# Top-32 attention feeding a relu-squared MLP on one core: how a block's scores lie in PSUM, which queue first loads k, and the numbers of the planner

## The chip, the core and the metric

The kernel runs on one core of a Trainium2 chip. Its engines work in parallel and wait for each other by semaphores: TensorE (PE in the profile, PEld its weight loads), VectorE (DVE), ScalarE (ACT), GpSimd (POOL) and the queue that issues most DMAs (SP). The metric is the device time of one execution in microseconds (us), lower is better.

## The reference

For 8 batches and 8 heads, with 576 positions of 64 values, attention keeps for each query only the 32 highest scores. A two-layer MLP follows on the 4608 tokens.

```python
scores = scale * np.matmul(q, k.transpose(0, 1, 3, 2))            # 576 x 576 for each head
kth = np.partition(scores, -top_k, axis=-1)[..., -top_k:-top_k + 1]
scores = np.where(scores >= kth, scores, -1000000000.0)
attn = np.exp(scores - np.max(scores, axis=-1, keepdims=True))
attn = attn / (np.sum(attn, axis=-1, keepdims=True) + 1e-09)
attn_out = np.matmul(attn, v)
...
h = x @ w_in                                                      # 4608 x 512 by 512 x 2048
return (np.maximum(h, 0.0) ** 2) @ w_out                          # 4608 x 2048 by 2048 x 512
```

## The kernel before

Attention is cut into 144 blocks. A block has 128 queries of two heads (or the last 64 queries of four heads, group Z) against all 576 keys, so 1152 scores per partition, in the order of `batch_order`. Each block goes through these steps; the letters are the names of the tiles in the profile.

- TensorE transposes the q and k of a head pair (`rq`, `rk`) and ScalarE copies them to `qk`. This is done once per pair.
- TensorE computes the scores into three PSUM banks `ss` (L408 is the line of every matmul, L411 of every transpose). The keys and queries of the first head lie in partitions 0 to 63, those of the second in 64 to 127, so the two heads use two halves of the array's rows. The 1152 scores lie in the three banks without a gap. The middle bank therefore holds the first head's last 64 scores beside 448 of the second head's. The matmul for these 64 is an operation of its own (`PIECES[1]`), and waits until the other four have ended.
- ScalarE copies all 1152 scores to SBUF in one instruction (`s`, L504). VectorE then takes the larger of each two scores that are half a row apart (`m`, L558), one from PSUM, the other from the copy. After that PSUM is free. There is one such `ss` for all blocks, so the next block's scores wait for this block's `m`.
- VectorE and GpSimd find the 32nd largest score (`kth`), working through maxima, minima and sums of pairs: `t` and `f` (L555) on GpSimd, `f`, `c` and `kth` (L563, L578, L582, L585) on VectorE.
- ScalarE builds a mask `w` (L593), TensorE transposes scores and mask (`ident,s` and `steep_bf,w`, 4 and then 5 chunks), and ScalarE takes the exponential (`p`, L626).
- TensorE multiplies with v (`vb,p`), ScalarE copies the result (`av`, L652), VectorE takes the reciprocal of the sums (`rzall`, L654), GpSimd scales (`x`, L656), TensorE transposes it (`ident_bf,x`) and ScalarE copies it to `xt`.

When a chunk of 128 to 512 tokens is complete, `feed` runs the MLP for it: `xt,win` on TensorE, relu and square on ScalarE or GpSimd (`g`), `wo,g` on TensorE, a copy `o` and a store. The MLP of a batch runs beside the attention of the next. The last chunks, two of 128 tokens, can only run at the end.

No order is written by hand. Every operation is given to `Plan.op` with an assumed duration and a priority, and `schedule` plays the program through with these numbers: an engine that is free takes the ready operation of the lowest priority. The order in which each engine's operations start in that play is the order of its instructions. `verdict` and a second program `again` behind a branch are not taken with these inputs.

Of the kernel before, what the change touches and what calls it, by code (L numbers as in the profile page):

```python
# [5 lines left out]
ALU = mybir.AluOpType  # L6
# [70 lines left out]
class Op:  # L77
    __slots__ = ("eng", "dur", "prio", "fn", "deps", "tiles", "takes", "n", "users", "start", "end",
                 "idx", "sem", "val", "ndma", "seq", "vc", "waits", "wars", "later", "nbf", "lk")
# [5 lines left out]
class Plan:  # L85
# [3 lines left out]
    def op(self, eng, dur, prio, fn, r=(), w=(), u=(), hold=(), take=(), after=(), order=(), sem=None, ndma=0, nbf=0.0, lk=False):  # L89
# [4 lines left out]
        o.eng, o.dur, o.prio, o.fn = eng, dur - (.05 if eng == "act" else 0), prio, fn  # L94
        o.sem, o.ndma, o.seq, o.nbf, o.lk = sem, ndma, len(self.ops), nbf, lk
# [22 lines left out]
    def schedule(self, t0=0.0, latency=0.12, own=0.07):  # L118
# [24 lines left out]
        while events:  # L143
            t = events[0][0]
            while events and events[0][0] <= t + 1e-9:
                _, _, kind, x = heapq.heappop(events)
                if kind == "end":
# [7 lines left out]
                    for v in x.users:  # L155
# [3 lines left out]
                        if left[v] == 0:  # L159
                            push(readyat[v], "ready", v)  # L160
# [47 lines left out]
class Emitter:  # L208
# [72 lines left out]
def bass_top_k_attn__then__act_relu_squared_kernel(  # L281
# [32 lines left out]
    STEP = 3.2  # L314

# [97 lines left out]
    def build(full, weights, pl):  # L413
        state = {"n": 0, "u": 0, "last": {}}
# [6 lines left out]
        def load_pair(b, hp, base):  # L421
            rq, rk, rv = tile("rq"), tile("rk"), tile("rv")

            def load(t, src):
                def fn():
                    r = at(t)
                    res = [nc.sync.dma_start(r[:, 0:4, h, :], src[b, 2 * hp + h, 0:512, :].rearrange(
                        "(tb p) d -> p tb d", p=P)) for h in range(2)]
                    res.append(nc.sync.dma_start(
# [14 lines left out]
            pl.op("sp", 2.3, base - 79.9, load(rk, k), w=[rk], take=[rk], sem=slot_sem, ndma=3)  # L444
# [16 lines left out]
            o_q = pl.op("pe", .55, base - 45, t4(tq, rq), r=[rq], w=[tq], take=[tq, qk])  # L461
            pl.op("pe", .55, base - 44.9, t4(tk, rk), r=[rk], w=[tk], take=[tk], order=[o_q])
# [5 lines left out]
            pl.op("gp", .9, base + 5, lambda: gp.tensor_copy(at(vb)[:, :, 0:D], at(rv)[:, :, :]),  # L468
# [3 lines left out]
        def top_k(gi, qks, tg):  # L472
# [461 lines left out]
```

## Time and profile before

| | |
|---|---|
| time, median of 3 runs | 969.63 us (967.36 to 971.03) |
| the profiled execution's own time | 972.14 us |
| its span, first to last instruction | 970.3 us |
| busy: PE, DVE, POOL, ACT | 887.8, 863.3, 750.4, 737.5 us |
| VectorE's first instruction of a block starts at | 15.86 us |
| VectorE's last `kth` ends at | 935.1 us |

The span is what the trace covers; the time also holds what lies around it. A busy TensorE is not TensorE at its peak, since matmuls overlap. The tables of stretches give the busy time of each engine in a piece of the span: an engine whose busy time is that of the piece had no room left.

### The profile page before, as it was taken

What the parts mean: (1) busy time and instruction counts of PE and PEld (TensorE: products, weight loads), DVE (VectorE), ACT (ScalarE), POOL (GpSimd) and SP (SyncE); (2) the same over time, 40 slices, a digit from 0 to 9 for tenths busy, and PEclk for the clock granted to TensorE, in tenths of its full rate; (3) what the DMA queues carried; (4) which work ended last, traced back from release to release, by engine and by line L of the source; (5) the groups of instructions that cost most, each with busy time, mean ns of one, the idle gap of its engine ahead of it and who ended that gap; (6) DMA issues with size and microseconds to landing.
All of it is one profiled execution on the core that took longest, in us unless ns stands there. A gap on an engine that the chain in (4) does not pass through costs nothing.

```text
span 970.3 us, 21522 instructions
## 1 busy us (share of the span) xinstructions
PE 887.8 (91%) x7650; PEld 620.2 (64%) x7650; DVE 863.3 (89%) x3269; ACT 737.5 (76%) x1133; POOL 750.4 (77%) x794
## 2 busy tenths in 40 slices
PE   5877789999799999999998999999999999999995
PEld 3655566777566666666766676666676655666654
DVE  1888799999999999999999999999999999786831
ACT  2555588898789877997789977998788879686752
POOL 5787688788877777778777787778799986599950
PEclk9976799999999999999999999999999999999998
DMA  6541153102310022001221112111111210000011
GB/s 155 143 124 67 44 136 79 38 15 60 87 38 15 20 67 71 16 15 38 59 49 39 39 35 74 25 39 38 36 48 26 53 33 23 23 11 13 22 34 37
DMA packets 126981, 48.15 MB, mean 50 GB/s; under 512 B 119184, under 2 KB 119184, under 8 KB 126864
## 3 DMA queue, kind: packets, MB, share of 16 engines
q1 hardware_dynamic: 126864, 46.69, 18.9%
q8 instruction: 62, 1.02, 0.4%
q14 instruction: 55, 0.45, 0.2%
HBM read 37.22 MB, written 9.44 MB: 48 GB/s over the span
## 4 chain that ended last, share of the span: by engine, by line
PE 44%; DVE 30%; POOL 10%; ACT 8%; issue 6%; DMA 0%; SPq 0%; POOLq 0%; DVEq 0%
PE ps L408 34%; PE ps L411 10%; DVE f L582 8%; DVE c L578 7%; DVE kth L585 6%; POOL f L555 6%; DVE m L558 5%; POOL t L555 3%; DVE f L563 3%; ACT p L626 3%; ACT s L504 2%; ACT w L593 1%; ACT g L706 1%; POOL x L656 1%; DMA rk<-in_k_dram 0%
## 5 line engine op out<-in xcount | busy, mean ns | idle before, releaser
L408 PE MATMUL ps<-qk 64*128 64x512 f32 (+6 forms) x1600 | 281.7, 413 | 30.0 <-DVE m L558 28.3
L408 PEld LDWEIGHTS ps<-qk 64*128 64x128 f32 (+1 forms) x1600 | 178.3, 183 | 141.6 <-DVE m L558 46.5
L582 DVE MATCH_REPLACE8 f<-c,f 128x104 f32<-128x104 f32 (+2 forms) x864 | 268.7, 320 | 0.0
L578 DVE MAX8 c<-f 128x8 f32<-128x104 f32 (+2 forms) x864 | 248.5, 325 | 0.2
L593 ACT ACTIVATE w<-s,kth 128x576 bf16<-128x576 f32 x288 | 220.6, 780 | 16.8 <-DVE kth L585 16.3
L555 POOL TENSOR_TENSOR t<-s 128x576 int32<-128x576 int32 x144 | 201.6, 1411 | 25.2 <-ACT s L504 25.1
L411 PE MATMUL ps<-ident,s 128*128 128x128 f32 x1296 | 204.1, 286 | 6.8 <-ACT w L593 6.3
L504 ACT COPY s<-ps 128x1152 f32<-128x1152 f32 x144 | 161.4, 1121 | 64.1 <-PE ps L408 62.8
L585 DVE MAX8 kth<-f 128x8 f32<-128x576 f32 x288 | 205.1, 751 | 2.4 <-POOL f L555 2.4
L555 POOL TENSOR_TENSOR f<-t,m 128x576 int32<-128x576 int32 x144 | 202.8, 1408 | 0.0
L626 ACT ACTIVATE p<-ps 128x1152 bf16<-128x1152 f32 x144 | 162.9, 1131 | 35.1 <-PE ps L408 34.3
L555 POOL TENSOR_TENSOR f<-t,f 128x288 int32<-128x288 int32 x144 | 114.5, 795 | 85.2 <-DVE f L563 82.6
L411 PEld LDWEIGHTS ps<-ident,s 128*128 128x128 f32 x1296 | 146.4, 144 | 35.5 <-ACT w L593 8.5
L558 DVE TENSOR_TENSOR m<-ps,s 128x576 f32<-128x576 f32 x144 | 107.9, 749 | 45.2 <-ACT s L504 41.9
L408 PE MATMUL ps<-wo,g 128*128 128x512 bf16 x576 | 143.4, 380 | 1.0 <-ACT xt L681 0.4
L408 PE MATMUL ps<-xt,win 128*128 128x512 bf16 (+3 forms) x704 | 134.3, 331 | 4.7 <-ACT xt L680 3.3
L408 PE MATMUL ps<-steep_bf,w 128*128 128x128 bf16 x1296 | 122.5, 223 | 0.0
L555 POOL TENSOR_TENSOR t<-m 128x288 int32<-128x288 int32 x144 | 115.0, 799 | 4.3 <-DVE m L558 4.3
L563 DVE TENSOR_REDUCE f<-m 128x288 f32<-128x576 f32 x144 | 106.4, 752 | 0.2
L706 ACT ACTIVATE g<-ps 128x512 bf16<-128x512 f32 (+1 forms) x152 | 85.3, 576 | 24.4 <-PE ps L408 23.8
L408 PEld LDWEIGHTS ps<-steep_bf,w 128*128 128x128 bf16 x1296 | 99.0, 100 | 3.9
L656 POOL TENSOR_TENSOR x<-av,rzall 128x256 bf16<-128x256 f32 (+1 forms) x88 | 47.1, 535 | 58.6 <-DVE rzall L654 58.2
(56 smaller groups left out, 750.7 us busy)
## 6 DMA issues: line engine op xcount, KB each, us to landing
rq<-in_q_dram SPq DMA_DIRECT2D x64, 128.0 KB, 2.5
rk<-in_k_dram SPq DMA_DIRECT2D x64, 128.0 KB, 2.6
rv<-in_v_dram SPq DMA_DIRECT2D x64, 128.0 KB, 2.4
out_dram<-o SPq DMA_DIRECT2D x31, 256.0 KB, 2.1
g<-in_moe_w_in_dram SPq DMA_DIRECT2D x8, 512.0 KB, 4.5
g<-in_moe_w_out_dram SPq DMA_DIRECT2D x8, 512.0 KB, 4.5
rv<-in_v_dram SPq DMA_DIRECT2D x96, 16.0 KB, 2.2
out_dram<-o SPq DMA_DIRECT2D x10, 128.0 KB, 2.3
```

Source lines behind the costliest of these rows:

```text
L408: return pe.matmul(o, l, r, start=start, stop=stop, skip_group_check=True)
L411: return pe.matmul(o, i, ident, is_transpose=True, skip_group_check=True, **kw)
L504: cp = pl.op("act", 1.15, tg - LEAD + 1, lambda: act.copy(at(st)[:, :, :].rearrange("p i c -> p (i c)"), wide(ss)), r=[ss], w=[st])
L555: return pl.op("gp", dur, prio, lambda: gp.tensor_tensor(o().bitcast(I32), x().bitcast(I32), y().bitcast(I32), op), **kw)
L558: dve(.7, lambda: vec.tensor_tensor(at(m)[:, :, :], wide(ss).rearrange("p (i c) -> p i c", i=2)[:, :, 0:HALF], at(st)[:, :, HALF:S], ALU.m ...
L563: big = dve(.67, lambda: vec.tensor_reduce(at(f)[:, :, 0:QUART], at(m)[:, :, :].rearrange("p i (a c) -> p i c a", a=2), AX.X, ALU.max), dp ...
L578: lambda i=i, t=t, c0=c0, c1=c1: vec.max(eighth(t, i), at(f)[:, i, c0:c1]),
L582: lambda i=i, t=t, c0=c0, c1=c1: vec.match_replace(at(f)[:, i, c0:c1], eighth(t, i), at(f)[:, i, c0:c1], NEG), hold=[f])]
L585: ks.append(chain(kth, i, prev[i] + [low], .665, lambda i=i: vec.max(eighth(kth, i), at(f)[:, i, :]), hold=[f]))
L593: pl.op("act", .77, tw + .8 * i, lambda i=i: act.activation(at(wt)[:, i, :], at(st)[:, i, :], ACTF.Relu, bias=kth[:, i, n:n + 1], scale=-1.0),
L626: pl.op("act", 1.15, tt + 1, lambda: act.activation(at(pt)[:, :, :].rearrange("p k q -> p (k q)"), wide(e), ACTF.Exp, scale=0.125), r=[e], ...
L706: return act.activation(at(g)[:, 0:kf * nt], bank(hh)[:, 0:kf * nt], ACTF.Relu)
```

## The change

The first head's 512 main scores get a bank, the second head's 512 get a bank, and the last 64 scores of both share the third. The four matmuls are now one operation: first the first head's 64 columns, then 512 and 512, then the second head's 64, ahead of which TensorE waits on a semaphore (`fence`) that the first of the four raises. ScalarE's copy becomes two instructions, 1024 and 128 columns, and `m` waits for both. The k of the first head pair is issued from ScalarE's queue. Of the loads, only those of v now wait for the zeroing of `rv`. The assumed durations are new; a reciprocal counts as ready 1.5 us later in the plan (`LATE`); the MLP chunks that wait for the last batch, except the very last one, get a lag of 10 in their priorities (`LAGL`, before 0).

```diff
-                            push(readyat[v], "ready", v)
+                            push(readyat[v] + v.late, "ready", v)
...
+    def via(self, plan, e):
+        for o in plan.order["sp"]:
+            if o.via == e:
+                assert not o.waits
+                for i in o.fn():
+                    i.then_inc(self.sem(o.idx[0]), 16)
+
     def emit(self, plan, e, eng):
         for o in plan.order[e]:
+            if o.via is not None:
+                continue
...
+    LATE = 1.5
+    LAGL = 10
...
+    def two(ap, step, n_):
+
+        return bass.AP(ap.tensor, ap.offset, [ap.ap[0], [step, 2], [1, n_]])
+
+    fence, fences = nc.alloc_semaphore("fence"), [0]
...
-            PIECES = [[(0, 0, 0, 512, True), (1, 576, 512, 64, True), (1, 640, 0, 384, False), (1, 1024, 384, 128, True)],
-                      [(0, 512, 512, 64, False)]]
-
-            def scores(part):
+            def scores():
                 o = wide(ss)
-                for h, to, c0, n_, first in PIECES[part]:
+                for h, to, c0, n_ in ((0, 1024, 512, 64), (0, 0, 0, 512), (1, 512, 0, 512), (1, 1088, 512, 64)):
                     x = at(qks[h])
+                    if to == 1088:
+                        pe.wait_ge(fence, fences[0])
                     ins = mm(o[:, to:to + n_], x[64 * h:64 * h + 64, 0, 128 * gi:128 * gi + 128],
-                             x[64 * h:64 * h + 64, 1, c0:c0 + n_], first)
+                             x[64 * h:64 * h + 64, 1, c0:c0 + n_], to != 1088)
+                    if to == 1024:
+                        fences[0] += 1
+                        ins.then_inc(fence, 1)
                 return ins
...
-            o_s = pl.op("pe", 1.2, tg - LEAD, lambda: fs(0), r=qu, w=[ss], take=[ss, st])
-            pl.op("pe", .15, tg - LEAD, lambda: fs(1), r=qu, w=[ss], after=[o_s])
-            cp = pl.op("act", 1.15, tg - LEAD + 1, lambda: act.copy(
-                at(st)[:, :, :].rearrange("p i c -> p (i c)"), wide(ss)), r=[ss], w=[st])
+            pl.op("pe", 1.25 if gi != Z else 1.4, tg - LEAD, scores if gi != Z else scores_z, r=qu, w=[ss], take=[ss, st])
...
+            cp = [pl.op("act", 1.1, tg - LEAD + 1, lambda: act.copy(
+                two(flat(), 640, 512), two(wide(ss), 512, 512)), r=[ss], w=[st]),
+                pl.op("act", .35, tg - LEAD + 1, lambda: act.copy(
+                    flat()[:, 512:640], wide(ss)[:, 1024:1152]), r=[ss], w=[st])]
...
-                dve(.7, lambda: vec.tensor_tensor(
-                    at(m)[:, :, :], wide(ss).rearrange("p (i c) -> p i c", i=2)[:, :, 0:HALF],
-                    at(st)[:, :, HALF:S], ALU.max), dp=-ME, r=[ss], hold=[st], after=[cp], w=[m], take=[m])
+                dve(.67, lambda: vec.tensor_tensor(
+                    at(m)[:, :, :], two(wide(ss), 736, HALF), two(flat()[:, HALF:], HALF, HALF), ALU.max),
+                    dp=-ME, r=[ss], hold=[st], after=cp, w=[m], take=[m])
...
-            rz = pl.op("dve", .1, tt + 4, lambda: vec.reciprocal(rzall[:, r0:r0 + nu], at(avs)[:, 0:nu, 64]), r=[avs])
+            rz = pl.op("dve", .1, tt + 4, lambda: vec.reciprocal(rzall[:, r0:r0 + nu], at(avs)[:, 0:nu, 64]), r=[avs], late=LATE)
...
-            lag = 0 if last else LAG
+            lag = 0 if end else LAGL if last else LAG
...
-        if o.eng == "sp":
+        if o.eng == "sp" and o.takes and o.takes[0].pool.name == "rv":
             o.deps.update(zeros)
```

The new numbers give every engine a new order. Three places are shown. The first is the start of the program. SP's first rows before (`g` is where a weight waits for its cast, 128x4x64 is the bulk of a q, k or v):

```order
L826 DMA g<-in_moe_w_in_dram 128x1024 x2
L427 DMA rq<-in_q_dram 128x4x64 x2
L429 DMA rq<-in_q_dram 64x2x64
L427 DMA rk<-in_k_dram 128x4x64 x2
L429 DMA rk<-in_k_dram 64x2x64
```

SP's first rows now; ScalarE's now begin with the first three loads of `rk`:

```order
L447 DMA rq<-in_q_dram 128x4x64 x2
L449 DMA rq<-in_q_dram 64x2x64
L456 DMA rv<-in_v_dram 128x4x64 x2
L460 DMA rv<-in_v_dram 64x64 x3
L447 DMA rq<-in_q_dram 128x4x64 x2
```

The two loads of `win` have moved from the first place to behind the fourth head pair, and k has left SP.

The second place is ScalarE between two copies of scores, in the second half of the program as it now stands:

```order
L533 COPY s<-ps 128x2x512
L683 COPY av<-ps 128x260
L535 COPY s<-ps 128x128
L737 ACTIVATE g<-ps 128x512
L624 ACTIVATE w<-s,kth 128x576
```

The small copy need not follow the large one: in 76 of the 144 blocks it does, in 68 something else stands between, mostly one copy to `av` or `xt`; in the 128th block it is 11 instructions, 10 of them of `g`.

The third place is TensorE at the end of the program. Before:

```order
L408 MATMUL ps<-wo,g 128x512 x12
L411 MATMUL ps<-ident_bf,x 128x128
L411 MATMUL ps<-ident,s 128x128 x5
L408 MATMUL ps<-steep_bf,w 128x128 x5
L408 MATMUL ps<-vb,p 128x65 x10
L411 MATMUL ps<-ident_bf,x 128x128
L847 MATMUL ps<-fone 1x3
L408 MATMUL ps<-xt,win 128x128 x64
L408 MATMUL ps<-wo,g 128x512 x16
```

And now:

```order
L428 MATMUL ps<-steep_bf,w 128x128 x5
L428 MATMUL ps<-wo,g 128x512 x4
L428 MATMUL ps<-xt,win 128x128 x16
...
L428 MATMUL ps<-wo,g 128x512 x8
L428 MATMUL ps<-vb,p 128x65 x10
L428 MATMUL ps<-wo,g 128x512 x12
L431 MATMUL ps<-ident_bf,x 128x128
L888 MATMUL ps<-fone 1x3
L428 MATMUL ps<-xt,win 128x128 x64
L428 MATMUL ps<-wo,g 128x512 x16
```

The last block's transposes now stand ahead of the work of the chunk before the last, and twelve `wo,g` stand between the last `vb,p` and the transpose of its result.

## Rows read from the trace of the kernel before

**Rows 1.** Stretches: length; busy PE, PEld, DVE, ACT, POOL; PEclk, DMA share, GB/s.

```profile
16.00:113.00 97.00, 74.61 (x484) 56.93 (x484) 74.43 (x273) 48.81 (x69) 71.23 (x71) 0.81 0.37 99
145.50:824.50 679.00, 645.20 (x5756) 450.33 (x5754) 667.50 (x2539) 570.08 (x872) 546.96 (x555) 1.00 0.17 42
826.00:936.00 110.00, 108.09 (x883) 71.09 (x882) 82.85 (x310) 78.11 (x129) 90.81 (x100) 1.00 0.05 18
```

**Rows 2.** VectorE's waits, 16 to 114 us: us in total, times, longest.

```profile
DVE m L558 <- ACT s L504: 35.5, 10, 15.9
```

**Rows 3.** VectorE's waits, 145 to 826 us.

```profile
DVE rzall L654 <- ACT av L652: 5.1, 12, 0.9
DVE m L558 <- ACT s L504: 2.9, 3, 2.1
```

**Rows 4.** VectorE's waits, 826 to 936 us.

```profile
DVE rzall L654 <- ACT av L652: 11.8, 7, 2.8
```

**Rows 5.** The chain that ended last, its first 22 us: start, length, what.

```profile
4.75 4.66 DMA rk<-in_k_dram
...
11.42 2.52 PE ps L408 x7
...
13.98 0.70 PE ps L408 x2
...
15.86 0.77 DVE m L558
...
19.18 1.45 PE ps L411 x6
```

**Rows 6.** SP's timeline, first us: start, length of the issue.

```profile
0.74 0.87 SPq L826 DMA_DIRECT2D g<-in_moe_w_in_dram  x2
...
4.75 1.66 SPq L429 DMA_DIRECT2D rk<-in_k_dram  x1
```

**Rows 7.** The page's DMA issues: count, KB each, median us to landing.

```profile
rk<-in_k_dram SPq DMA_DIRECT2D x64, 128.0 KB, 2.6
```

**Rows 8.** TensorE's timeline near 891 us, one block's scores: start, length.

```profile
890.64 1.36 PE L408 MATMUL ps<-qk 64*128 64x512 f32 x8
891.94 1.04 PE L408 MATMUL ps<-wo,g 128*128 128x512 bf16 x4
892.90 0.43 PE L408 MATMUL ps<-qk 64*128 64x64 f32 x2
893.26 0.66 PE L411 MATMUL ps<-ident,s 128*128 128x128 f32 x4
```

**Rows 9.** TensorE's groups by shape, 890.6 to 891.1 us: count, busy, mean ns.

```profile
L408 PE MATMUL ps<-qk 64*128 64x512 f32 x1 | 0.7, 693 | 0.0
L408 PE MATMUL ps<-qk 64*128 64x384 f32 x1 | 0.5, 539 | 0.0
```

**Rows 10.** Groups by shape, whole span: busy, mean ns, idle before them.

```profile
L504 ACT COPY s<-ps 128x1152 f32<-128x1152 f32 x144 | 161.4, 1121 | 64.1 <-PE ps L408 62.8
L466 ACT COPY qk<-ps 128x128 f32<-128x128 f32 x32 | 8.8, 274 | 0.1
```

**Rows 11.** Groups by shape, 826 to 970 us.

```profile
L408 PE MATMUL ps<-qk 64*128 64x512 f32 x26 | 14.6, 641 | 0.4 <-DVE m L558 0.4
```

**Rows 12.** Table of stretches round 265 us and 956 us, columns as in rows 1.

```profile
258.00:264.00 6.00, 3.89 (x35) 3.03 (x36) 6.00 (x27) 5.01 (x8) 6.00 (x6) 1.00 0.43 98
264.00:270.00 6.00, 6.00 (x55) 3.54 (x53) 4.54 (x16) 1.39 (x3) 3.98 (x6) 0.72 0.22 48
...
954.00:958.00 4.00, 3.67 (x41) 3.60 (x40) 0.88 (x5) 0.94 (x3) 0.00 (x0) 0.57 0.02 6
```

**Rows 13.** TensorE's timeline at the end: start, length, [idle before, who ended it].

```profile
952.27 0.49 PE L408 MATMUL ps<-vb,p 128*128 128x65 bf16 x10 [1.22 <-ACT p L626]
953.80 0.23 PE L411 MATMUL ps<-ident_bf,x 128*128 128x128 bf16 x1 [1.03 <-POOL x L656]
...
954.49 5.18 PE L408 MATMUL ps<-xt,win 128*128 128x128 bf16 x64
```

More of the change, by code (lines that the diff above doesn't have):

```diff
@@ L78 @@
     __slots__ = ("eng", "dur", "prio", "fn", "deps", "tiles", "takes", "n", "users", "start", "end",
-                 "idx", "sem", "val", "ndma", "seq", "vc", "waits", "wars", "later", "nbf", "lk")
+                 "idx", "sem", "val", "ndma", "seq", "vc", "waits", "wars", "later", "nbf", "lk", "late",
+                 "via")
 ENGS = ("pe", "act", "dve", "gp", "sp")
@@ L87, in __init__, with op @@
         self.ops = []
-    def op(self, eng, dur, prio, fn, r=(), w=(), u=(), hold=(), take=(), after=(), order=(), sem=None, ndma=0, nbf=0.0, lk=False):
+    def op(self, eng, dur, prio, fn, r=(), w=(), u=(), hold=(), take=(), after=(), order=(), sem=None, ndma=0, nbf=0.0, lk=False, late=0.0, via=None):
         o = Op()
-        o.eng, o.dur, o.prio, o.fn = eng, dur - (.05 if eng == "act" else 0), prio, fn
-        o.sem, o.ndma, o.seq, o.nbf, o.lk = sem, ndma, len(self.ops), nbf, lk
+        o.eng, o.dur, o.prio, o.fn = eng, dur - (.1 if eng == "act" else 0), prio, fn
+        o.sem, o.ndma, o.seq, o.nbf, o.lk, o.late, o.via = sem, ndma, len(self.ops), nbf, lk, late, via
         o.takes = list(take)
@@ L443, in load_pair @@
             pl.op("sp", 2.3, base - 80, load(rq, q), w=[rq], take=[rq], sem=slot_sem, ndma=3)
-            pl.op("sp", 2.3, base - 79.9, load(rk, k), w=[rk], take=[rk], sem=slot_sem, ndma=3)
+            via = "act" if not full and not state["pairs"] else None
+            state["pairs"] += 1
+            pl.op("sp", 2.3, base - 79.9, load(rk, k, nc.scalar if via else nc.sync), w=[rk], take=[rk], sem=slot_sem,
+                  ndma=3, via=via)
             pl.op("sp", 2.3, base - 70, loadv, w=[rv], take=[rv], sem=slot_sem, ndma=5)
@@ L487, in scores, with scores_z @@
                     ins = mm(o[:, to:to + n_], x[64 * h:64 * h + 64, 0, 128 * gi:128 * gi + 128],
[L488 removed]
+                             x[64 * h:64 * h + 64, 1, c0:c0 + n_], to != 1088)
+                    if to == 1024:
+                        fences[0] += 1
+                        ins.then_inc(fence, 1)
                 return ins
[L491 removed]
+            def scores_z():
                 o = wide(ss)
[L493 removed]
+                for i in range(2):
@@ L494, in scores_z @@
                     x = at(qks[i])
-                    for h in range(2):
-                        ins = mm(o[64 * h:64 * h + 64, to:to + n_], x[64 * h:64 * h + 64, 0, 512:576],
-                                 x[64 * h:64 * h + 64, 1, c0:c0 + n_], first)
+                    for to, c0, n_, first in ((1024 + 64 * i, 512, 64, i == 0), (512 * i, 0, 512, True)):
+                        for h in range(2):
+                            ins = mm(o[64 * h:64 * h + 64, to:to + n_], x[64 * h:64 * h + 64, 0, 512:576],
+                                     x[64 * h:64 * h + 64, 1, c0:c0 + n_], first)
@@ L709, in feed @@
                 w_ = kf * nt
-                ho = pl.op("pe", kf * 4 * (nt / 2200 + .01), tf + lag, fh, r=[xt], w=[hh], take=[hh, g], after=weights,
+                ho = pl.op("pe", .03 + kf * 4 * (nt / 2340 + .002), tf + lag, fh, r=[xt], w=[hh], take=[hh, g], after=weights,
                       nbf=tf if not last else 0)
@@ L829, in setup, with warm @@
                                  r=[s]))
+        for i in range(int(WARM / .45)):
+            t = Tile(psum)
+            def warm(t=t):
+                for _ in range(2):
+                    ins = mm(bank(t), ident_bf[:, :], ident_bf[:, :].unsqueeze(1).broadcast_to([P, 4, P]), True)
+                return ins
+            pl.op("pe", .45, 1e5, warm, w=[t], take=[t], after=[i2], nbf=.45 * i)
         return [i1], pre, zeros, weights
```

39 lines of the change are left out of this document (20 added, 19 removed).

## The prediction

> **What bounds the kernel now.** I read the table of stretches first, then VectorE's waits in each stretch, then the chain of waits at both ends. The table [rows 1] shows three stages with different limits. From 145 to 824 us VectorE is busy 667.5 of 679.0 us, while TensorE has 34 us to spare: VectorE is the bound, and whatever other engines save there is worth nothing. Its waits there are small: 5.1 us for the result that a reciprocal needs, 2.9 us for a block's scores [rows 3]. From 826 to 936 us it is the other way round: TensorE is busy 108.1 of 110.0 us and VectorE has 27.2 us of holes, because the MLP work of two batches falls in there. From 16 to 113 us neither is full. VectorE has 22.6 us of holes and waits for scores, at a mean granted clock of 0.81 [rows 1, 2]; The longest, 15.9 us, is the wait for the very first block, ahead of 16. The waits of 16 to 113 for scores are therefore 35.5 - 15.9 = 19.6 us in nine pieces.
>
> So the change can win at the start and at the end. In the middle it can only lose.
>
> **The start of the program.** The chain starts with the last piece of k: issued at 4.75 us, landed 4.66 later, at 9.41 [rows 5]. Ahead of it SP issued two loads of 512 KB for the weights [rows 6]. They now come behind the fourth pair, and k's three loads go out on ScalarE's queue beside q's. The two weight loads took 0.87 us to issue, so about 0.45 each; three k loads from about 0.74 on are out by about 2.1. With this start's 4.66 to landing that is 6.8, with the median of 2.6 [rows 7] 4.7. I take 5.7, since q and k still move together and only the weights are gone: **-3.7 us** (bounds -2.6 and -4.7).
> [...]
> ScalarE's other first work, a table load, is pushed back behind the three issues by these 1.35 us; it is covered by the wait for the landing, and would cost that much without it. The MLP first uses the weights some 20 blocks later in TensorE's order, so their delay is covered by those blocks.
>
> **A block's scores.** At the end of the program one block's four matmuls take 1.36 us. The fifth, alone, takes 0.43, and 0.36 from its start to that of the next work [rows 8]. At half the clock, at the start, the fifth takes 0.70 on the chain [rows 5]. Does the new group stay at 1.36? In the old one the first head streams 512 columns and the second 64 + 384 + 128 = 576; in the new one each has 576. If the two heads' matmuls overlap as now, the longer half is what it was, and the group is unchanged. That they overlap, rows 9 show: in the first half microsecond there is one pass of the first head's 512 columns (each fp32 matmul is two) and already a pass of the second head's 384, which the program issues later. I take 1.36. The other bound is no overlap at all, at most twice that. The semaphore ahead of the last 64 is raised by the first and shortest matmul, so it should be up long before its turn: nothing, since the two 512s cover it. Without that cover all that stands behind on TensorE would wait too.
>
> **ScalarE's copy.** 1152 columns take 1121 ns, 128 take 274 [rows 10]. A straight line between them gives 1015 for 1024, so the two copies take 1289, **0.17 us more per block**, 24 us of ScalarE's time in all. In the middle ScalarE is busy 570 of 679 us [rows 1] and VectorE waits for scores in three places only, so I cost it at nothing there. At the start it lies on the chain. The first block's `m` thus moves from 15.86 by -3.7 - 0.70 + 0.17, to 11.6: **-0.5** beside the -3.7.
>
> **The other holes of the start.** Nine waits for scores remain. Each had the fifth matmul at up to 0.70 in it, less 0.17 for the copy, so 4.8 us. In some, the next pair's transposes (1.45 us at 19.18, [rows 5]) stood between the four matmuls and the fifth. They can't any more; I count two of them, 2.9. Together **-8 us**. The bounds are -3, if only half of the fifth matmuls lay on the path and no transposes, and -15, if most of the 19.6 vanishes.
>
> **The middle.** A later reciprocal can win at most the 5.1 us [rows 3]. What is late next is `x` on GpSimd, and then the MLP, which has a lag of its own in the plan. Against that stands a fuller ScalarE and a TensorE with more holes. I take **-2** (bounds -5 and +6).
>
> **The end.** Of 512-column passes 26 remain after 826 us [rows 11], so 13 blocks, each 0.36 less on a full TensorE: **-4.7** (bounds 0 and 13 x 0.43 = -5.6). VectorE's 11.8 us of waits for reciprocals there [rows 4] are no term of their own, since TensorE sets the pace. Behind the last block TensorE stood still for 1.22 and 1.03 us [rows 13]. Then the clock fell (0.57 in that stretch, [rows 12]), and 64 matmuls of the last chunk took 5.18. The new order puts twelve `wo,g` into the second gap and the last transposes earlier, so that exponential and result are covered. I take **-2.5**: 2.25 of gap and something of the clock (bounds 0 and -3.5).
>
> **The sum.** -3.7 - 0.5 - 8 - 2 - 4.7 - 2.5 = -21.4 us. The profiled execution's own time, 972.14, would become 950.7. That execution lies 2.5 us over the median of the runs shown; from the median, 969.63, it is **948 us**. Adding the bounds gives -34 to about +0, so 935 to 969.
>
> **The rivals.**
> *More is won* (933 us): the fifth matmul is gone from every loop in which scores wait for `m` and `m` for scores, so the start follows VectorE almost at once. For it: 19.6 us of waits in nine places. Against it: the half clock there. The sum at its bounds, 969.6 - 34 = 935, and a little of the 27.2 us of holes at the end. Chance 0.15.
> [...] Chance 0.14. [...]
> *The heads don't overlap* (960 us): with the first head's 64 and 512 ahead of the second's 512, the second could wait until the first head's second pass has started. The group then grows by one pass, at most 0.69 [rows 9], and eats the 0.43; only the load, the reciprocals and the last order are left, some 9 us. Against it: rows 9. Chance 0.08. [...]
> *Slower* (976 us): ScalarE becomes what VectorE waits for. In 68 blocks an instruction stands between the two copies, so `m` is later by up to 0.17 + 0.38 or more, `ss` stays taken as long, and everything behind `m` on VectorE waits. To cancel the win it takes 21.4 us, or 0.2 us of VectorE's time in each of the 110 or so blocks of the middle; 976 needs 0.25. For it: in the middle ScalarE has only 109 us left of 679. Against it: three waits for scores there, 2.9 us. Chance 0.06.
>
> **Chances.** Forecast 0.57 (its own range 940 to 956), more 0.15, clock 0.14, no overlap 0.08, slower 0.06. The range that leaves out no more than 2 in 10 is 934 to 962. A measurement of this kernel tells about 0.5% from no change, 4.8 us. Under 964.8: the forecast, the win and nearly all of the two at 960, so 0.89; within 0.5%: 0.06; slower 0.05.
>
> **What would show it.** Right: the first `m` near 11.6 us; one group of eight passes per block, 1.3 to 1.4 us at full clock; holes of VectorE from the first `m` to 113 us near 14 us; VectorE busy 98% or more of the middle, as now; TensorE full from about 815 us and the last gaps gone. Wrong: a score group of 1.8 or more; `m` waiting for the second copy in dozens of places; granted clock at half in stretches of the middle; first `m` after 13 us.

## The result, and the profile after

The changed kernel takes **933.08 us** (median; 930.32 to 938.05) beside 970.33 for the kernel before on the same chip: a ratio of 0.9627 [0.9577, 0.9676], 37 us less. The profiled execution is the shortest of its four, 930.32 us with a span of 928.2, so a stretch of it can flatter the change by a few us; where it does, other kernels with the same start stand beside it. Ratios leave out four executions at a lower granted clock (one of e2 at 0.958, one of e8 at 0.648 and 1187 us, two of e11 at 0.959 and 0.958), and the medians hold them.

The first part of the page of the changed kernel; 77 of its 7330 matmuls are missing from the record, so that TensorE's busy time is some us too low:

```profile
PE 810.1 (87%) x7253; PEld 565.7 (61%) x7330; DVE 864.2 (93%) x3269; ACT 742.8 (80%) x1277; POOL 750.3 (81%) x794
```

VectorE has as much to do as before (863.3), TensorE some 64 us less than its 887.8 (a kernel that differs only in the lag, e5 below, has a full record with 823.3), in a span that is 42 us shorter. The table of stretches of the changed kernel, for the cuts of [rows 1]; the third, where VectorE finishes, now lies 36 us earlier:

```profile
16.00:113.00 97.00, 69.72 (x620) 53.72 (x620) 93.67 (x356) 66.15 (x109) 89.96 (x91) 0.91 0.52 137
145.50:824.50 679.00, 609.33 (x5532) 423.58 (x5594) 673.22 (x2547) 578.56 (x990) 550.25 (x560) 0.99 0.17 42
790.00:900.00 110.00, 106.51 (x917) 70.91 (x929) 92.44 (x352) 84.37 (x155) 98.48 (x110) 1.00 0.05 18
```

VectorE's holes between 16 and 113 us fell from 22.6 to 3.3 us. In the middle VectorE was the bound and still is; TensorE's busy time there fell by 36 us (62 of the missing matmuls lie there), which buys nothing. At the end TensorE is still the bound (106.5 of 110), but VectorE gets through more blocks in the same time (92.4 busy, before 82.9).

Equal cuts of time hold different blocks. So the next two tables are cut at the same blocks (counted from 0): from the start of the `m` of block 0 to that of block 16, from there to block 120, and from there to the end. Before:

```profile
15.86:125.50 109.64, 83.66 (x576) 63.44 (x576) 87.01 (x321) 57.10 (x79) 81.78 (x82) 0.83 0.36 96
125.50:748.10 622.60, 589.26 (x5325) 417.71 (x5326) 614.80 (x2345) 522.78 (x798) 504.16 (x512) 1.00 0.19 46
748.10:970.30 222.20, 208.00 (x1728) 134.53 (x1725) 161.43 (x605) 153.80 (x253) 157.22 (x169) 0.99 0.10 27
```

And after:

```profile
12.39:102.70 90.31, 63.70 (x534) 49.08 (x535) 85.32 (x317) 57.68 (x94) 83.22 (x84) 0.91 0.51 133
102.70:725.70 623.00, 552.72 (x5097) 390.96 (x5149) 619.56 (x2347) 532.72 (x915) 507.49 (x514) 0.99 0.19 47
725.70:928.20 202.50, 187.83 (x1604) 121.51 (x1626) 159.32 (x607) 148.51 (x264) 154.44 (x166) 0.99 0.08 24
```

That is the whole account of the two profiled spans, which lie 42 us apart (the medians 37): 3.5 us up to the first `m`, 19.3 in the first 16 blocks, nothing in 104 blocks of the middle, 19.7 in the last 24 blocks and what follows them.

VectorE's waits after, 16 to 114 us, to be read beside [rows 2] (of which 19.6 us lie in this stretch):

```profile
DVE m L589 <- ACT s L535: 2.6, 4, 1.4
DVE f L613 <- POOL f L586: 2.3, 1, 2.3
```

145 to 826 us, beside [rows 3]; the waits for reciprocals are gone:

```profile
DVE f L613 <- POOL f L586: 3.1, 5, 1.5
DVE m L589 <- ACT s L535: 1.9, 4, 0.8
```

The chain of waits of the changed kernel up to its first `m`, beside [rows 5]:

```profile
1.79 3.89 DMA rq<-in_q_dram
...
5.82 1.96 PE ps L431 x8
...
7.79 0.58 ACT qk L488
...
8.60 2.55 PE ps L428 x6
...
11.17 1.01 ACT s L533
12.18 0.18 ACT s L535
...
12.39 0.77 DVE m L589
```

The last piece is now one of q. It landed at 5.68 us, 3.73 earlier than k's did. But all eight large transposes now stand behind that landing, where before those of q ran while k was on its way: from landing to scores it takes 2.92 us instead of 2.01. Before, the four of the first q began 1.35 us ahead of k's landing at 9.41:

```profile
8.06 1.12 PE L411 MATMUL ps<-ident,rq 128*128 128x128 f32 x4 [8.06 <-DMA rq<-in_q_dram]
```

TensorE's timeline near 601 us, one block's scores and the next work, beside [rows 8]:

```profile
600.82 1.34 PE L428 MATMUL ps<-qk 64*128 64x64 f32 x8
602.09 0.66 PE L431 MATMUL ps<-ident,s 128*128 128x128 f32 x4
```

All eight passes take 1.34 us, 1.27 to the start of the next work. Before it was 1.30 and then 0.36 for the fifth matmul: 0.39 us a block less. The first tenth of a microsecond, 600.80 to 600.90, by shape, beside [rows 9]:

```profile
L428 PE MATMUL ps<-qk 64*128 64x512 f32 x1 | 0.7, 693 | 0.0
L428 PE MATMUL ps<-qk 64*128 64x64 f32 x1 | 0.3, 320 | 0.0
```

A pass of 512 columns already runs beside the first pass of the first head's 64. I take it for the second head's: the second pass of the 64 starts only in the next tenth, and the first head's own 512 stands behind that one in the program. e6, which holds the second head back, fits: there the group takes 3.02 us. ScalarE's two copies in the groups by shape (busy, mean ns, idle before them), beside [rows 10]:

```profile
L533 ACT COPY s<-ps 128x1024 f32<-128x1024 f32 x144 | 146.5, 1017 | 84.2 <-PE ps L428 83.8
L535 ACT COPY s<-ps 128x128 f32<-128x128 f32 x144 | 40.7, 282 | 0.0
```

The end of TensorE's timeline after, beside [rows 13]:

```profile
910.24 0.48 PE L428 MATMUL ps<-vb,p 128*128 128x65 bf16 x10
910.55 2.75 PE L428 MATMUL ps<-wo,g 128*128 128x512 bf16 x12
913.14 0.22 PE L431 MATMUL ps<-ident_bf,x 128*128 128x128 bf16 x1
914.07 0.19 PE L888 MATMUL ps<-fone 128*1 128x3 f32 x2 [0.71 <-ACT o L768]
914.19 3.75 PE L428 MATMUL ps<-xt,win 128*128 128x128 bf16 x64
```

The gaps of 1.22 and 1.03 us have become one of 0.71, and the last 64 matmuls take 3.75 us instead of 5.18.

### The profile page after: what moved, and what is told of

Same layout as the page of the kernel before. It is cut to its first block, busy times and chain, and to the rows that moved or that the text cites. A ratio compares the mean times of both kernels' runs of the same rounds, so it can differ in the third digit from the quotient of the medians.

```text
span 928.2 us, 20946 instructions
## 1 busy us (share of the span) xinstructions
PE 810.1 (87%) x7253; PEld 565.7 (61%) x7330; DVE 864.2 (93%) x3269; ACT 742.8 (80%) x1277; POOL 750.3 (81%) x794
## 4 chain that ended last, share of the span: by engine, by line
DVE 45%; PE 35%; ACT 14%; issue 3%; DMA 1%; POOL 1%; SPq 0%; DVEq 0%
PE ps L428 27%; DVE f L613 13%; DVE kth L616 10%; DVE c L609 10%; PE ps L431 9%; DVE m L589 6%; DVE f L594 5%; ACT p L657 5%; ACT w L624 3%; ACT s L533 2%; ACT g L737 1%; ACT g L751 1%; DMA rq<-in_q_dram 1%; ACT xt L711 0%; ACT qk L488 0%
## 5 line engine op out<-in xcount | busy, mean ns | idle before, releaser
L609 DVE MAX8 c<-f 128x8 f32<-128x104 f32 (+2 forms) x864 | 243.7, 321 | 0.1
L428 PE MATMUL ps<-qk 64*128 64x64 f32 (+3 forms) x1280 | 213.9, 454 | 32.8 <-DVE m L589 31.6
L586 POOL TENSOR_TENSOR t<-s 128x576 int32<-128x576 int32 x144 | 203.1, 1413 | 17.7 <-ACT s L535 17.6
L431 PE MATMUL ps<-ident,s 128*128 128x128 f32 x1296 | 200.2, 283 | 16.0 <-ACT w L624 15.4
L533 ACT COPY s<-ps 128x1024 f32<-128x1024 f32 x144 | 146.5, 1017 | 84.2 <-PE ps L428 83.8
L616 DVE MAX8 kth<-f 128x8 f32<-128x576 f32 x288 | 203.4, 748 | 1.6 <-POOL f L586 1.6
L428 PEld LDWEIGHTS ps<-qk 64*128 64x128 f32 (+1 forms) x1280 | 129.2, 180 | 110.2 <-DVE m L589 48.1
L428 PE MATMUL ps<-xt,win 128*128 128x512 bf16 (+3 forms) x674 | 126.8, 324 | 13.7 <-ACT g L737 7.4
L428 PE MATMUL ps<-wo,g 128*128 128x512 bf16 x529 | 134.2, 379 | 4.5 <-ACT xt L711 1.2
L589 DVE TENSOR_TENSOR m<-ps,s 128x576 f32<-128x576 f32 x144 | 107.5, 747 | 19.3 <-ACT s L535 16.9
L737 ACT ACTIVATE g<-ps 128x512 bf16<-128x512 f32 (+1 forms) x152 | 87.2, 581 | 20.2 <-PE ps L428 19.7
L428 PEld LDWEIGHTS ps<-xt,win 128*128 128x128 bf16 x704 | 57.7, 98 | 51.8 <-ACT g L737 11.8
```

The lines of the kernel that those rows point to most:

```text
L431: return pe.matmul(o, i, ident, is_transpose=True, skip_group_check=True, **kw)
L533: cp = [pl.op("act", 1.1, tg - LEAD + 1, lambda: act.copy(two(flat(), 640, 512), two(wide(ss), 512, 512)), r=[ss], w=[st]), pl.op("act", . ...
L586: return pl.op("gp", dur, prio, lambda: gp.tensor_tensor(o().bitcast(I32), x().bitcast(I32), y().bitcast(I32), op), **kw)
L589: dve(.67, lambda: vec.tensor_tensor(at(m)[:, :, :], two(wide(ss), 736, HALF), two(flat()[:, HALF:], HALF, HALF), ALU.max), dp=-ME, r=[ss] ...
L609: lambda i=i, t=t, c0=c0, c1=c1: vec.max(eighth(t, i), at(f)[:, i, c0:c1]),
L616: ks.append(chain(kth, i, prev[i] + [low], .665, lambda i=i: vec.max(eighth(kth, i), at(f)[:, i, :]), hold=[f]))
```

## The experiments

The theory after the result: the layout is the core, the loads add 3 to 4 us, and the rest of the change only arranges. The rival: the new numbers of the planner carry a good part. This table holds, for each kernel cut at the same blocks as above, the start of the first `m` and the length of the three stretches in its profiled execution, the granted clock of the first stretch, and the median of its runs (us):

| kernel | first `m` | 0 to 16 | clock there | 16 to 120 | 120 to end | time |
|---|---|---|---|---|---|---|
| before | 15.86 | 109.6 | 0.83 | 622.6 | 222.2 | 968 to 970 |
| the change | 12.39 | 90.3 | 0.91 | 623.0 | 202.5 | 933.1 |
| e1, layout only | 15.04 | 96.5 | 0.89 | 620.6 | 215.6 | 946.7 |
| e2, all but the layout | 13.13 | 101.6 | 0.87 | 630.6 | 215.4 | 965.6 |
| e3, old loads | 15.11 | 96.6 | 0.86 | 623.1 | 203.4 | 936.7 |
| e4, `LATE` 0 | 12.68 | 97.8 | 0.84 | 634.3 | 204.1 | 948.6 |
| e5, no lag | 12.64 | 96.7 | 0.86 | 621.5 | 204.8 | 933.3 |
| e6, heads serial | 15.49 | 153.1 | 0.65 | 752.3 | 238.6 | 1158.2 |
| e7, copies adjacent | 12.38 | 96.4 | 0.88 | 627.6 | 203.1 | 936.1 |
| e8, TensorE busy early | 10.65 | 97.6 | 0.79 | 623.2 | 203.0 | 936.6 |
| e9, old durations | 12.62 | 91.3 | 0.91 | 619.3 | 215.7 | 943.0 |
| e10, `LATE` 3 | 12.47 | 96.1 | 0.84 | 632.2 | 203.1 | 947.3 |
| e11, serial fifth | 13.12 | 116.3 | 0.74 | 643.1 | 214.0 | 979.8 |
| e12, `LATE` 1.7 | 12.45 | 97.0 | 0.84 | 623.3 | 206.4 | 941.5 |

Each stretch comes from one execution. In the first 16 blocks the change and e9 have the highest granted clock, 0.91, and take 90 and 91 us; the seven others with the new layout and without added matmuls or waits were granted 0.84 to 0.89 and take 96 to 98.

**e1: the layout alone**, with the kernel before's loads and planner.

```diff
-            o_s = pl.op("pe", 1.2, tg - LEAD, lambda: fs(0), r=qu, w=[ss], take=[ss, st])
-            pl.op("pe", .15, tg - LEAD, lambda: fs(1), r=qu, w=[ss], after=[o_s])
+            pl.op("pe", 1.25 if gi != Z else 1.4, tg - LEAD, scores if gi != Z else scores_z, r=qu, w=[ss], take=[ss, st])
...
+            cp = [pl.op("act", 1.05, tg - LEAD + 1, lambda: act.copy(
+                two(flat(), 640, 512), two(wide(ss), 512, 512)), r=[ss], w=[st]),
+                pl.op("act", .3, tg - LEAD + 1, lambda: act.copy(
+                    flat()[:, 512:640], wide(ss)[:, 1024:1152]), r=[ss], w=[st])]
```

> The kernel before with the new score layout alone: four matmuls in one operation with the fence, two copies, the new m; loads, reciprocals, lag and all other numbers of the planner as before. Theory (the fifth matmul left every loop of scores, copy and m): most of the 37 us comes with it, so 940 to 948 us, VectorE's holes from its first m to 113 us at 5 to 9 us instead of 22.6, first m at about 15.3. Rival (the new orders are what won): 960 to 968 us and holes of 18 us or more.

946.73 us, ratio 0.9768 [0.973, 0.9805]: 22 us of the 37. The start gains 13 us, the end 6.6. VectorE's holes from 16 to 113 us are 10.9 us, a little more than expected. Its end, TensorE's timeline:

```profile
929.61 0.49 PE L414 MATMUL ps<-vb,p 128*128 128x65 bf16 x10 [0.62 <-ACT o L751]
931.13 0.23 PE L417 MATMUL ps<-ident_bf,x 128*128 128x128 bf16 x1 [1.03 <-POOL x L670]
...
931.81 5.19 PE L414 MATMUL ps<-xt,win 128*128 128x128 bf16 x64
```

A gap of 1.03 us and the slow 64 matmuls, 5.19 us, are still there. The layout doesn't touch them.

**e2: everything but the layout.**

```diff
-            pl.op("pe", 1.25 if gi != Z else 1.4, tg - LEAD, scores if gi != Z else scores_z, r=qu, w=[ss], take=[ss, st])
+            o_s = pl.op("pe", 1.25, tg - LEAD, lambda: fs(0), r=qu, w=[ss], take=[ss, st])
+            pl.op("pe", .33, tg - LEAD, lambda: fs(1), r=qu, w=[ss], after=[o_s])
+            cp = pl.op("act", 1.17, tg - LEAD + 1, lambda: act.copy(
+                at(st)[:, :, :].rearrange("p i c -> p (i c)"), wide(ss)), r=[ss], w=[st])
```

> The changed kernel with the old score layout: five matmuls, one copy, the old m; loads, late reciprocals, lag and the planner's new numbers stay (the two score operations count 1.25 and 0.33 us in the plan). Theory: 957 to 965 us, that is the load (3.5) and a few us of reciprocals and end; the holes of the start stay near 18 us. Rival (the new orders won): 936 to 946 us.

965.55 us, ratio 0.9966 [0.9938, 0.9994]: 3 us are left of the 37. But these 3 are a balance. In the profiled executions, which lie 9.5 us apart, the first `m` comes 2.7 us earlier than before, the first 16 blocks take 8.0 us less and the end 6.8 less, while the middle takes 8.0 more. Its waits of VectorE, 110 to 790 us:

```profile
DVE m L581 <- ACT s L527: 11.7, 12, 3.2
```

The same view of the kernel before:

```profile
DVE rzall L654 <- ACT av L652: 5.1, 12, 0.9
DVE m L558 <- ACT s L504: 4.2, 4, 2.1
```

The waits for reciprocals are gone here too, but those for scores have grown by more, 7.5 us. That the new numbers need the room on TensorE that the layout makes fits this; it was not tried by itself.

**e3: the old loads.**

```diff
-            via = "act" if not full and not state["pairs"] else None
+            via = None
...
-        if o.eng == "sp" and o.takes and o.takes[0].pool.name == "rv":
+        if o.eng == "sp":
```

> The changed kernel with the first k on SP and all loads behind the zeroing, as before. Theory (the load is worth what the first m moved, 3.5 us, and nothing more): 936 to 938 us, first m at 15 to 16 us. Rival (an earlier start also brings the clock up earlier and so removes holes): 941 us or more.

936.65 us, ratio 0.9654 [0.961, 0.9698], 3.6 more than the change. The first `m` is at 15.11; the weights' loads are again SP's first. By its time alone e3 can't be told from the change (the intervals overlap, and e7 lies 3.0 off), but the first `m` comes 2.7 us later. So the loads are worth about 3 us, as in the theory.

**e4: the reciprocal not late.**

```diff
-    LATE = 1.5
+    LATE = 0.0
```

> The changed kernel with reciprocals ready at once in the plan (0 for 1.5 us). Theory: the 5.1 us of waits of the middle come back and no more, 936 to 939 us. Rival (nothing: the waits are covered since TensorE now has room): 932 to 934 us.

948.58 us, ratio 0.9794 [0.9741, 0.9848]. The theory fell: taking this one number away costs 15 us. VectorE's waits, 110 to 790 us:

```profile
DVE rzall L685 <- ACT av L683: 8.3, 13, 1.3
DVE m L589 <- ACT s L535: 4.6, 3, 3.4
```

The middle takes 634.3 us, 11 more than with 1.5.

**e5: no lag, and e7: the two copies as one operation.**

```diff
-    LAGL = 10
+    LAGL = 0
```

> The changed kernel with the lag of the last batch's MLP chunks at 0 as before. Theory (TensorE sets the pace of the end, and only the sum of its work counts, not whose turn it is): 932 to 935 us. Rival (the lag lets the last blocks' attention pass and so brings the last kth forward): 937 to 942 us, last kth later by 3 us or more against the last first-step m of the middle.

```diff
-            cp = [pl.op("act", 1.1, tg - LEAD + 1, lambda: act.copy(
-                two(flat(), 640, 512), two(wide(ss), 512, 512)), r=[ss], w=[st]),
-                pl.op("act", .35, tg - LEAD + 1, lambda: act.copy(
-                    flat()[:, 512:640], wide(ss)[:, 1024:1152]), r=[ss], w=[st])]
+            def copies():
+                act.copy(two(flat(), 640, 512), two(wide(ss), 512, 512))
+                return act.copy(flat()[:, 512:640], wide(ss)[:, 1024:1152])
+
+            cp = [pl.op("act", 1.35, tg - LEAD + 1, copies, r=[ss], w=[st])]
```

> The changed kernel with both copies of a block in one operation of the plan, so that nothing stands between them on ScalarE. Theory (m is not on the path of the middle, so what stands between costs nothing): 931 to 935 us. Rival (a late m holds up the scores where TensorE is full): 926 to 929 us.

e5: 933.32 us, ratio 0.9601 [0.955, 0.9652]; e7: 936.06 us, 0.9626 [0.9568, 0.9684]. Neither can be told from the change, so neither the lag nor the instructions between the two copies do anything that a measurement sees.

**e6: the heads one after the other.** The second head's 512 waits for the first's to end, and the second head's last 64 for its own 512, instead of for the first head's 64.

```diff
-                    if to == 1088:
+                    if to == 512 or to == 1088:
...
-                    if to == 1024:
+                    if to in (0, 512):
```

> The changed kernel with the second head's 512 columns waiting for the first head's 512 to end, so that the two heads don't overlap. Theory (they overlap in the changed kernel; that is what holds the group at about 1.36 us): the group grows to 2.2 us or more, TensorE has not the room for 144 times that, 965 to 1000 us. Rival (they already run one after the other): 933 to 937 us, group unchanged.

1158.23 us, ratio 1.1919 [1.1824, 1.2014]. TensorE's timeline, one block and the next work:

```profile
603.20 3.02 PE L428 MATMUL ps<-qk 64*128 64x64 f32 x8
606.15 0.66 PE L431 MATMUL ps<-ident,s 128*128 128x128 f32 x4
```

From start to next start 2.95 us instead of 1.27. The edit reaches the 128 blocks that are not of group Z: 1.68 us more for each makes 215 us, and TensorE becomes the bound: from block 16 to 120 it is busy 709.2 of 752.3 us, VectorE 626.4. The time grows by 225; the granted clock over the whole run fell too, to between 0.93 and 0.94. So in the changed kernel the heads do overlap, and the price of losing that was set far too low (965 to 1000 us). The 1.68 holds both waits, not the lost overlap alone, and the middle doesn't hide it.

**e8: TensorE kept busy from the start**, eight matmuls of the identity that the reference doesn't need.

```diff
-    WARM = 0
+    WARM = 1.9
```

> The changed kernel with eight more matmuls of 512 columns on TensorE ahead of the first transposes, while it waits for q; their results are not used. Theory (the holes left at the start come from the half clock up to 17 us): full clock some 10 us earlier, first m 1 to 2 us earlier, 929 to 932 us. Rival (the first blocks are bound by VectorE anyway, and the extra work delays the transposes): 933 to 936 us.

936.6 us, ratio 0.9641 [0.9581, 0.97]: no gain. Its table of stretches:

```profile
10.00:15.00 5.00, 2.30 (x15) 1.51 (x14) 1.96 (x5) 2.95 (x7) 4.30 (x5) 1.00 0.54 121
15.00:20.00 5.00, 3.95 (x15) 3.11 (x16) 4.46 (x19) 1.38 (x3) 2.97 (x4) 0.56 0.57 129
...
45.00:50.00 5.00, 4.24 (x19) 3.07 (x18) 2.31 (x6) 1.91 (x3) 2.74 (x3) 0.50 0.54 112
```

The first block's scores take 1.35 us instead of 2.50 on TensorE's timeline, and the first `m` comes at 10.65, 1.7 us earlier, as the theory had it. But TensorE is then busy 2.3 of 5 us and in the next 5 the granted clock is 0.56; from 45 to 50 us it is 0.50. From there to block 16 it takes 97.6 us, about 1 us more than e5 or e7, at 0.79 of the clock: over half of the early 1.7 us is lost again.

The half clock of the first blocks, which the theory and the prediction name, stands in no table: the granted clock reads 1.00 up to 48 us before and up to 20 us after. It is read from times. In the kernel before, a block's four matmuls took 2.51 us at 23.06, 1.36 at 36.20, and 2.51 again at 89.24, where the granted clock was 0.50; the fifth took 0.70 on the chain of the first block and 0.69 at 93.14. In the changed kernel a block's scores take 2.50 us at 8.60 and 13.20, and 1.35 at 18.55.

**e9: the old durations in the planner**, everything else as in the change (three of fifteen lines).

```diff
-            o_t = pl.op("pe", .68, tt, lambda: flip([0, 128, 256, 384], 0), r=[st, wt], w=[e], take=[e, pt])
-            pl.op("pe", .84, tt + .1, lambda: flip([640, 768, 896, 1024, 512], 4), r=[st, wt], w=[e], order=[o_t])
+            o_t = pl.op("pe", .75, tt, lambda: flip([0, 128, 256, 384], 0), r=[st, wt], w=[e], take=[e, pt])
+            pl.op("pe", .95, tt + .1, lambda: flip([640, 768, 896, 1024, 512], 4), r=[st, wt], w=[e], order=[o_t])
...
-                    pl.op("pe", .9, to + lag + step * sub, fo,
+                    pl.op("pe", 1.0, to + lag + step * sub, fo,
```

> The changed kernel with the old assumed durations of all operations that both versions share (the late reciprocal, the lag, the loads and the layout stay). Theory: what the planning brought is the late reciprocal, as its removal alone cost 15 us; the other durations moved by 0.1 us or less and bring nothing. Then 932 to 940 us, and VectorE waits for no reciprocal between 145 and 790 us. Rival: the measured durations bring a good part, since every engine's order hangs on them: 944 us or more, with the waits spread over m and rzall.

942.99 us, ratio 0.9733 [0.9699, 0.9767]. The theory fell, and the rival's bound was missed by 1 us: the durations bring 10 us, but not by VectorE's waits (from 145 to 790 us they are 0.8 for scores and 0.6 for reciprocals). From block 120 to the end, the table of stretches:

```profile
723.20:938.90 215.70, 197.76 (x1675) 125.77 (x1672) 160.35 (x605) 153.36 (x277) 156.84 (x167) 0.99 0.10 28
```

The same stretch of e5, which has the new durations and no matmul missing from its record:

```profile
730.80:935.60 204.80, 190.51 (x1628) 121.59 (x1626) 159.66 (x607) 148.76 (x264) 154.96 (x166) 0.99 0.08 24
```

With the old durations the end takes 215.7 us, as in e1; with the new ones 10.9 less: TensorE is busy 7.3 us less there, and idle 14.3 instead of 17.9. Forty-seven fewer matmuls lie in this stretch. In e9 it still holds 16 large transposes each of `rq` and `rk`, in e5 and in the change 4 each. Of e9's groups by shape in that stretch:

```profile
L431 PE MATMUL ps<-ident,rq 128*128 128x128 f32 x16 | 2.5, 284 | 0.1
L431 PE MATMUL ps<-ident,rk 128*128 128x128 f32 x16 | 2.3, 275 | 0.9 <-DMA rk<-in_k_dram 0.9
```

Twelve of each, 3.5 us, six small ones, and sixteen matmuls of the MLP (8 `wo,g`, 4 `xt,win`, 4 `xz,win`) run earlier with the new durations, in the middle, where TensorE has room.

**e10 and e12: the reciprocal 3.0 and 1.7 us late.**

```diff
-    LATE = 1.5
+    LATE = 3.0
```

> The changed kernel with the reciprocal 3.0 us late in the plan instead of 1.5. Theory: its waits are already gone from the middle at 1.5, so there is nothing more to win there: 930 to 938 us, no different from the changed kernel. Rival: a later reciprocal makes the scaled result late, and with it the MLP, which ends the program: 940 us or more, with TensorE short of work after the last kth.

```diff
-    LATE = 1.5
+    LATE = 1.7
```

> The changed kernel with the reciprocal 1.7 us late in the plan. Nothing was late at 1.5 in the middle, so 0.2 us more can't matter by its mechanism, but the plan is played through anew and the order of every engine changes. Theory: 1.5 stands for where the reciprocal's result really arrives, and the time depends on it smoothly: between the 933 of 1.5 and the 947 of 3.0, so 932 to 937 us. Rival: the 14 to 15 us that 0 and 3.0 lost are mostly luck of the order, which any other number draws anew: 939 to 948 us, with waits for m in the middle and the stretch from the 16th to the 120th block over 628 us.

e10: 947.25 us, ratio 0.9777 [0.9733, 0.982]; e12: 941.47 us, 0.9697 [0.9654, 0.974]. The theory fell in both. e10 loses 9 us in the middle, where VectorE now waits for scores, 110 to 790 us:

```profile
DVE m L589 <- ACT s L535: 9.6, 5, 4.6
```

The rival's time came true, but its reason did not: 29.9 us lie behind the last `kth`, in the change 29.0. e12 has nothing of that kind. Its middle is as the change's, and its profile shows only 3.4 us over that of e5 in all, while the medians lie 8 apart. Where the rest goes can't be read from one execution; the granted clock, below, goes with it.

**e11: the fifth matmul back**, in the new layout and the new order, into columns that nobody reads.

```diff
+                fences[1] += 1
+                ins.then_inc(fence2, 1)
+                pe.wait_ge(fence2, fences[1])
+                x = at(qks[0])
+                return mm(ps32[:, BASE[ss.pool.name] + 2, 128:192], x[0:64, 0, 128 * gi:128 * gi + 128], x[0:64, 1, 512:576], False)
```

> The changed kernel with a fifth matmul of the first head's last 64 keys behind each of the 128 blocks that are not of group Z, into 64 unused columns of the third bank, which waits until the other four have ended, as the old layout's did; it adds work that the reference doesn't have. The order of all operations stays as it is. Theory: the wait on TensorE itself was the price, 0.36 us a block: TensorE's busy time grows by some 45 us, the start loses 8 to 12 us, the 24 blocks from the 120th on lose 8, and the time is 948 to 958 us. Rival: the price was that other work could get between the four and the fifth, since it was an operation of its own; that isn't so here, and the time is 934 to 941 us.

979.83 us, ratio 1.0081 [1.0041, 1.0121]. The theory had the cause right, the places in part, and the size too small: it expected 948 to 958 us. TensorE's timeline:

```profile
599.47 1.87 PE L429 MATMUL ps<-qk 64*128 64x64 f32 x10
601.26 0.66 PE L432 MATMUL ps<-ident,s 128*128 128x128 f32 x4
```

From start to next start 1.79 us, 0.52 more than in the change and 0.13 more than the kernel before paid. There the planner could put other work between the four and the fifth (four `wo,g` in [rows 8]), which covered the wait for the four to end; here nothing does. Where nothing stood between in the kernel before, it paid as much, 1.78 us:

```profile
258.48 1.85 PE L408 MATMUL ps<-qk 64*128 64x512 f32 x10 [0.18 <-DVE m L558]
260.26 0.66 PE L411 MATMUL ps<-ident,s 128*128 128x128 f32 x4
```

The start loses 26 us, the middle 20 and the end 11.5. Their sum is too high by some 12 us: the profiled execution, 988.6 us, is the longest of ten, and the change's the shortest of four. So a serial fifth, with nothing in its gap, costs more than the whole change wins.

## Why the prediction was right, and where its sizes were off

Faster was right. The forecast of 948 lies 15 us over the measured time, which lies just under the low end of the range. The places of the gain, the start and the end, were right, and so were the mechanisms named there; two terms of the sum were too small, and what a new order moves out of the end was counted for the last block alone.

**The load, -3.7, and the first block, -0.5.** The landing moved by -3.73, as taken. The first `m` moved by 3.5 instead of 4.2. The scores and copies gave 0.65 (4.44 to 3.79 from the scores' start to `m`), but the transposes of q had been hidden by the wait for k, and that cover went with the wait (+0.9): where the prediction put the change of the first block at -0.5, it came out at +0.3. The piece that ended the wait was issued 2.96 us earlier and took 3.89 us instead of 4.66 to land, the other 0.77 of the 3.73. Whether the second queue or the missing weight loads shortened that was not told apart. e3, where k follows the weights on SP again, gives 3.6 us of time back and moves the first `m` by 2.7.

**The other holes of the start, -8: mis-sized.** The first 16 blocks gained 19.3 us in the profiled execution, and some 13 in seven other kernels of the table with the new layout, which take 96 to 98 us there instead of 109.6 (e9, at 91.3, is nearer the change). So some 6 of the 19.3 go with the higher clock of two executions. e1 shows that the layout alone brings 13. It need not be the only thing that can: e2, without it, gained 8.0, and why stays open. The step that failed is "each had the fifth matmul at up to 0.70 in it, less 0.17", over nine waits: it took the fifth's own length as all that a block could win. e11 adds nothing but the fifth and its wait, and loses 18 to 26 us in these blocks, where 0.52 us in each of 16 would be 8.3 at the granted clock of 1.00 that the block shown there had. That the clock adds to it, as TensorE's longer waits go with a lower granted clock there (0.74 in e11's stretch, 0.91 in the change's), fits but was not tried by itself.

**The middle, -2.** 0 came out. The waits for reciprocals are gone, and VectorE is busy 619.6 of 623.0 us, but it spends 4.8 us more on the same blocks. That it got no worse hung on the order: with `LATE` at 0 or 3.0 the middle loses 11 or 9 us, past the bound of +6.

**ScalarE's copy** costs 1017 + 282 ns, 0.18 us more a block (0.17 predicted), and nothing in the middle. The rival "slower" fell with e7: instructions between the copies cost nothing that a measurement sees.

**The end, -4.7 and -2.5: mis-sized.** 19.7 came out. The layout alone gave 6.6 (e1), of which 13 blocks at 0.36 were 4.7. What the term of the last gaps named came about as sized: two gaps of 2.25 us in all became one of 0.71, and the 64 matmuls took 1.43 less, 3.0 together for 2.5. But with the old durations the end is 11 to 13 us longer (e9), by the order that they give. The step that failed is "the last gaps", which took from the new order only what it showed at the last block. TensorE sets the pace from the last blocks to the end, so what the planner moves from there into the middle is won: 7.3 us of work between e9 and e5, with 3.6 of idle time; counting the transposes of `rq` and `rk` behind block 120 in both orders would have shown some 3.5 us of it.

**The rivals.** "More is won" gave the time, 933, by half of its reason: the start does follow VectorE more closely, but the larger part of what I missed lay at the end. The rival of the clock, that a lower one takes the win back (chance 0.14), did not come: the granted clock from 16 to 113 us rose from 0.81 to 0.91, and in the middle it is 0.99. That a lower clock would cost 12 us, and so make 960 of the 948, was the author's estimate, and no run shows it. The clock did fall a little: from block 16 to 120 the granted clock was 1.00 before, 0.99 in the change and 0.98 in e1, e4, e7, e9 and e10. That need not cost the middle much: e1 and e9, at 0.98, have its two shortest times in the table. There is still the fall of [rows 12], now at about 238 us. The table of stretches of the changed kernel there:

```profile
229.00:235.00 6.00, 3.35 (x28) 2.50 (x28) 6.00 (x24) 3.96 (x7) 4.86 (x6) 1.00 0.01 1
235.00:241.00 6.00, 4.61 (x26) 3.53 (x26) 6.00 (x23) 2.20 (x3) 3.96 (x4) 0.72 0.01 3
241.00:247.00 6.00, 5.32 (x44) 2.90 (x44) 4.49 (x22) 1.70 (x4) 4.96 (x6) 0.72 0.23 52
```

VectorE loses 1.5 us (4.49 of 6.0), as much as before, but now it waits for GpSimd's `f` and not for scores. "The heads don't overlap" is ruled out by the 1.34 us of the group and by the pass of 512 in its first tenth of a microsecond; e6, which holds the heads further apart than this rival did, shows that it could cost more than a pass.

**What the parts are worth.** Put alone into the kernel before, the layout gives 22 us (e1). Taken out of the change, the loads cost 3.6 (e3) and the new durations 10 (e9), which makes 36 of 37. But taken out of the change the layout costs 32 (e2): without it the rest is worth 3 us. So the rival was right that the numbers carry a good part, but they do it only together with the layout. `LATE` can't be added to these. With the new durations, 0, 1.5, 1.7 and 3.0 give 948.6, 933.1, 941.5 and 947.3; with the old durations and 1.5 it is 943.0, about what e1 less the loads would be. That late reciprocals remove waits is shown by e4. But how much of the 10 to 15 us is this and how much is that 1.5 happens to give a good order stays open: e12 moves the number by 0.2 and loses 8 us without a wait that would explain it. The granted clock goes with these times: the four executions of e5 had 0.980 to 0.989 over the span, e12's 0.974 to 0.978, e4's 0.965 to 0.970, e10's 0.961 to 0.971, and within the change 930.3 us came at 0.985 and 938.1 at 0.972. Whether the order lowers the clock or the clock alone makes these differences is not shown.

## What to carry to other kernels

Price a stall on an engine by the stretch: the same 0.39 us a block was worth nothing in 104 blocks where VectorE is the bound, and all of it, with more behind it, where the blocks wait for each other or TensorE is full. Where a planner orders the work, compare the two orders at the border of the stage that its bound ends, and count how much of that engine's work lies behind it in each; a tenth of a microsecond in an assumed duration moved 7 us of it here. And don't read a planner's number from one good result: neighbours of 1.5 lose 8 to 15 us, so a value is worth only what its neighbours confirm. Nor does a part have one price: the layout was worth 22 us put in first and 32 taken out last.

## What the runs showed of the hardware

A matmul that waits for the matmuls just ahead of it on its own engine costs more than its columns: 64 columns cost 0.52 us with nothing in the gap (e11), 0.36 with other work in it [rows 8]. An estimate from [rows 11], two passes at an eighth of 641 ns, is 0.16. No run here takes that wait out of a block of two heads, so what it guards against is not shown.

Two heads in different halves of the array's rows overlap even though the program issues a 512 of each behind the other: 1.27 us a block, and 2.95 when the second's 512 is held until the first's has ended, and its 64 until its own 512 has. In the kernel before, a pass of the second head's 384 ran beside the first pass of the first head's 512 [rows 9]; in the changed one a pass of 512, which I take for the second head's, ran beside the first of the first head's 64.

Eight matmuls of the identity ahead of the first transposes brought the first block's scores from 2.50 to 1.35 us, and the second's too, while the granted clock read 1.00 with them and without. It was 0.56 in the 5 us after a stretch in which TensorE was busy 2.3 of 5 (e8).
